# In the whole pairs the row sums' small additions, minima and squares run on GpSimd, in three instructions, in place of two on VectorE

## The chip, the cores and the metric

The kernel runs on one core of a Trainium2 chip. The metric is the device time of one execution in microseconds. The core's engines run side by side, each through its own instructions in a fixed order, and wait for one another through semaphores: TensorE (PE, with its weight loads as PEld), VectorE (DVE), ScalarE (ACT), GpSimd (POOL), and SyncE (SP), whose queue issues the DMA transfers.

## The reference

An attention with a threshold, whose output goes through a two-layer network with a leaky activation. There are 8 batches of 8 heads with 576 positions of 64 numbers, and 4608 tokens of 512 numbers.

```python
scores = scale * np.matmul(q, k.transpose(0, 1, 3, 2))
thresh = np.max(scores, axis=-1, keepdims=True) - tau
scores = np.where(scores >= thresh, scores, -1000000000.0)
scores = scores - np.max(scores, axis=-1, keepdims=True)
attn = np.exp(scores)
attn = attn / (np.sum(attn, axis=-1, keepdims=True) + 1e-09)
out = np.matmul(attn, v)                  # then (batch, seq, head) as x
h = x @ w_in
g = np.maximum(h, 0.0) + alpha * np.minimum(h, 0.0)
y = g @ w_out
```

## The kernel before

Two heads of a batch make a pair; there are 32 pairs. A pair is worked in nine units of 128 score rows (`UNITS`), so the attention has 288 units, and a loop over cycles `i` emits the work around one unit per cycle. The order in which it emits is the order in which PE, DVE, ACT and POOL run their instructions (`manual_schedule`); SP's queue is ordered by the scheduler.

For a unit, PE computes the scores `s` in one of two PSUM buffers (line 441), DVE takes the row maximum `nmx` (line 456), ACT computes the exponentials `p` and the threshold `thr` (lines 464 and 469), and DVE masks `p` by the threshold and accumulates the row sum into a column of the pair's tile `sm` (line 476, called the mask below). The mask is the last reader of `s`, so PE may fill that buffer again only behind it. PE transposes `p` (line 485), and ACT or DVE carry the result to SBUF (lines 558 and 561 in the whole pairs). PE multiplies it with the values (`av`, line 620).

A pair's nine columns of sums become the factors by which its output is scaled: `recip` computes `rv` from `sm`, PE transposes `rv` one cycle later (`rp`, line 643), ACT copies it (line 647), SP sends it out to DRAM and back as `rb`, and POOL multiplies the output `xa` with it, five cycles behind the transpose.

The first five pairs (0 to 4) are "whole" (`WHOLE = 5`): their probabilities are kept in one float32 part, with a share `SHARE / S` added to each (lines 558 and 561), and their factor is min(sum, 1) times the sum, inverted. The other 27 pairs split the probabilities in two parts, and their factor is the sum inverted. `recip` of a whole pair runs in cycle `o + 9`, where `o` is the pair's first cycle: the last mask of the pair lies one cycle earlier, and the mask and a row maximum of the next pair are emitted ahead of `recip`.

In the same cycles the weights of the second network are decoded from 64-bit words (`Split64`): loads, ACT lines 139, 140 and 160, the DVE lines 143 (clamp), 146 (shift), 151 (sign) and 156 (power) on SBUF tiles of 128x512, and on POOL the products, differences and sums of lines 164 to 168, each in two halves of 128x256, which the trace shows at line 77, the line of the helper (`wri`, `wti`, `wi` and `wro`, `wto`, `wo` are the tiles). POOL also subtracts the rounded keys and queries of a coming pair (`kl` and `qt`).

From cycle 45 on the network's first layers are woven between the units, and after the attention its other passes follow, with PE as the engine that all of them use.

Of the kernel before, what the change touches and what calls it, by code (L numbers as in the profile page):

```python
# [10 lines left out]
F32 = mybir.dt.float32  # L11
# [5 lines left out]
ALU = mybir.AluOpType  # L17
# [4 lines left out]
P = 128  # L22
# [58 lines left out]
def tile_masked_attention_moe(  # L81
# [11 lines left out]
    nc = tc.nc  # L93
# [173 lines left out]
    ap1 = at.enter_context(tc.tile_pool(name="ap1", bufs=1))  # L267
# [35 lines left out]
    class Pair:  # L303
# [329 lines left out]

        def recip(self):
            self.rv = ap1.tile([P, 9], F32, tag="rv", name=f"rv{self.pi}", bufs=2)
            nc.vector.tensor_scalar(self.rv, self.sm, 1e-9, None, op0=ALU.add)
            if self.whole:
                nc.vector.scalar_tensor_tensor(self.rv, self.rv, 1.0, self.rv, op0=ALU.min, op1=ALU.mult)
            nc.vector.reciprocal(self.rv, self.rv)

        def rturn(self):
# [617 lines left out]
```

## Time and profile before

| | |
|---|---|
| median of 3 runs | 1360.91 us (1358.39 to 1362.42) |
| profiled execution | 1360.37 us, span 1358.6 us |
| PE busy | 1324.9 us, 98% of the span |
| PEld busy | 1162.3 us, 86% |
| DVE busy | 973.6 us, 72% |
| ACT busy | 842.4 us, 62% |
| POOL busy | 970.8 us, 71% |

The span runs from the first to the last instruction of one profiled execution; its own time is 1.8 us longer. A busy time counts the instructions' own durations, waits inside an instruction included. Times in the rows below are microseconds from the start of the span.

### The profile page before, as it was taken

Reading aid. Unit: us, or ns where it says so; the run is one execution under the profiler, and the core shown is the slowest. Engines: PE = TensorE matmul, PEld = TensorE weight load, DVE = VectorE, ACT = ScalarE, POOL = GpSimd, SP = SyncE. Lnnn points to the kernel's source line nnn. Section 1 sums busy time; section 2 is a strip of 40 time slices with the busy share of each in tenths; the row PEclk is TensorE's granted clock in tenths of the full one; section 3 lists DMA queues with packets and bytes.
Section 4 is the critical chain, followed back from the end, with each engine's and each line's share of the span. In section 5 each row is a group of like instructions: output and inputs, shape, how many; then the busy total and the mean of one; then the engine's idle time right before and its main releaser. Section 6 shows DMA issues by size and latency. Waiting matters only on the chain.

```text
span 1358.6 us, 24051 instructions
## 1 busy us (share of the span) xinstructions
PE 1324.9 (98%) x8041; PEld 1162.3 (86%) x8041; DVE 973.6 (72%) x1843; ACT 842.4 (62%) x1910; POOL 970.8 (71%) x1369
## 2 busy tenths in 40 slices
PE   6988999999999999999999999999999999999999
PEld 4655799999999999999999999988888888888887
DVE  6989889889888888888888874665565744333332
ACT  7888888888888888888888873433332321211110
POOL 3766899899889898988988985775665754433431
PEclk9999999999999999999999999999999999999999
DMA  8653544644544645545445414345555443343222
GB/s 241 183 160 104 152 131 121 166 128 120 160 134 124 165 127 142 140 132 144 141 136 146 117 51 127 109 132 170 183 164 196 134 145 124 109 152 113 93 78 86
DMA packets 113595, 186.04 MB, mean 137 GB/s; under 512 B 16608, under 2 KB 47872, under 8 KB 113472
## 3 DMA queue, kind: packets, MB, share of 16 engines
q1 hardware_dynamic: 113152, 183.92, 46.2%
q8 instruction: 64, 1.05, 0.3%
q10 hardware_dynamic: 320, 0.59, 0.2%
q14 instruction: 59, 0.48, 0.1%
HBM read 104.41 MB, written 37.90 MB: 105 GB/s over the span
## 4 chain that ended last, share of the span: by engine, by line
PE 83%; DVE 6%; ACT 6%; POOL 1%; DMA 1%; issue 1%; ACTq 0%; SPq 0%; POOLq 0%; DVEq 0%
PE acca L256 12%; PE pha L226 12%; PE s L441 10%; PE phc L226 9%; PE av L620 8%; PE accc L256 8%; PE accb L256 7%; PE phb L226 7%; PE t L485 7%; DVE p L476 2%; DVE nmx L456 2%; PE tk L501 1%; PE accc L981 1%; ACT p L464 1%; ACT xh L205 1%
## 5 line engine op out<-in xcount | busy, mean ns | idle before, releaser
L456 DVE TENSOR_REDUCE nmx<-s 128x1 f32<-128x576 f32 x288 | 217.2, 754 | 67.8 <-PE s L441 65.3
L256 PE MATMUL acca<-wo,ga 128*128 128x512 f32 x756 | 224.1, 415 | 0.9 <-ACT xb L631 0.9
L476 DVE SCALAR_TENSOR_TENSOR p<-s,thr,p 128x576 f32<-128x576 f32 x256 | 206.6, 807 | 4.5 <-ACT thr L469 4.4
L464 ACT ACTIVATE p<-s,nmx 128x576 f32<-128x576 f32 x256 | 189.8, 741 | 8.7 <-DVE nmx L456 8.4
L441 PE MATMUL s<-kh,qst 128*128 128x288 f32 x640 | 141.6, 311 | 27.9 <-DVE p L476 16.2
L250 POOL TENSOR_TENSOR gc<-ptc,gc 128x512 fp32r<-128x512 f32 x45 | 58.1, 1292 | 144.0 <-ACT gc L247 144.0
L226 PE MATMUL pha<-xh,wi 128*128 128x256 f32 x784 | 157.9, 285 | 0.2 <-ACT pra L239 0.2
L485 PE MATMUL t<-ident,p 128*128 128x128 f32 x1024 | 154.5, 273 | 0.0
L247 ACT ACTIVATE gc<-ptc 128x512 fp32r<-128x512 f32 x45 | 28.4, 632 | 196.8 <-DVE ptc L951 196.8
L256 PEld LDWEIGHTS acca<-wo,ga 128*128 128x128 f32 x756 | 133.5, 190 | 19.1 <-ACT xb L631 1.4
L441 PEld LDWEIGHTS s<-kh,qst 128*128 128x128 f32 x640 | 100.1, 191 | 54.6 <-issue 26.4
L226 PEld LDWEIGHTS pha<-xh,wi 128*128 128x128 f32 x784 | 128.0, 190 | 6.5 <-ACT pra L239 3.6
L441 PE MATMUL s<-kl,qst 128*128 128x288 f32 x640 | 133.1, 298 | 0.0
L485 PEld LDWEIGHTS t<-ident,p 128*128 128x128 f32 x1024 | 124.4, 141 | 1.3 <-DVE e L551 1.0
L942 POOL TENSOR_TENSOR homexl<-homexr,homexh 128x512 fp32r<-128x512 f32 (+1 forms) x84 | 103.2, 1247 | 22.1 <-ACT homexh L941 22.0
L226 PE MATMUL phc<-homexh,wi 128*128 128x512 f32 x360 | 112.5, 389 | 0.0
L226 PE MATMUL pha<-xl,wi 128*128 128x256 f32 x392 | 110.7, 283 | 0.0
L578 POOL TENSOR_TENSOR rt<-kw,rt 64x128 fp32r<-64x128 f32 x216 | 97.8, 453 | 17.3
L256 PE MATMUL accc<-wo,gc 128*128 128x512 f32 x480 | 110.1, 389 | 0.0
L250 POOL TENSOR_TENSOR ga<-pta,ga 128x256 fp32r<-128x256 f32 x126 | 96.0, 763 | 18.5 <-ACT ga L247 10.1
L256 PEld LDWEIGHTS accc<-wo,gc 128*128 128x128 f32 x480 | 90.1, 188 | 18.7
L551 DVE TENSOR_TENSOR eo<-t,eo 128x512 fp32r<-128x512 f32 (+1 forms) x162 | 94.7, 598 | 12.7 <-ACT eo L547 11.5
(160 smaller groups left out, 3345.2 us busy)
## 6 DMA issues: line engine op xcount, KB each, us to landing
kr<-in_k_dram SPq DMA_DIRECT2D x31, 320.0 KB
rb<-rvd SPq DMA_DIRECT2D x64, 144.0 KB
xs<-xa SPq DMA_DIRECT2D x32, 288.0 KB
pinb<-part SPq DMA_DIRECT2D x36, 256.0 KB
part<-obb SPq DMA_DIRECT2D x36, 256.0 KB
pinc<-part SPq DMA_DIRECT2D x36, 256.0 KB
out_dram<-obc SPq DMA_DIRECT2D x35, 256.0 KB
qr<-in_q_dram SPq DMA_DIRECT2D x31, 288.0 KB
```

What stands on the lines that cost most here:

```text
L226: nc.tensor.matmul(ph[:, :n], w[:, c, :], xx[:, c, :n], start=(c == 0 and ti == 0), stop=(c == NCC - 1 and ti == 2),)
L250: nc.gpsimd.tensor_tensor(g[:, 1, :n], t[:, :n], f(g[:, 0, :n]), op=ALU.subtract)
L256: nc.tensor.matmul(acc[:m, :], gg[:, g, o : o + m], w, start=(first and ti == 0), stop=(last and ti == 2))
L441: nc.tensor.matmul(ps[:, h, :288], w, kk[:, a + h * 288 : a + (h + 1) * 288], start=(ki == 0 and i == 0), stop=(ki == 1 and i == n - 1),)
L456: nc.vector.tensor_reduce(self.nmx[:, j : j + 1], self.S[u][0][:, :, :288], axis=AX.XY, op=ALU.max, negate=True)
L464: nc.scalar.activation(pj, ps[:, :, :288], AF.Exp, bias=nmx[:, j : j + 1], scale=1.0)
L476: nc.vector.scalar_tensor_tensor(pj, ps[:, :, :288], thr[:, j : j + 1], pj, op0=ALU.is_ge, op1=ALU.mult, accum_out=self.sm[:, c : c + 1])
L485: nc.tensor.transpose(tb[:, c, :], pt[:, j, j * D + c * P : j * D + (c + 1) * P], ident)
L551: nc.vector.tensor_tensor(dst[1], ps, f(dst[0]), op=ALU.subtract)
L578: nc.gpsimd.tensor_tensor(lo, r, f(hi), op=ALU.subtract)
L620: nc.tensor.matmul(pa[:m, :n], w, x, start=(part == 0 and c == 0), stop=c == NKC)
L942: self.low.tensor_tensor(xl[:, c, :n], xr[:, c, :n], f(xh[:, c, :n]), op=ALU.subtract)
```

## The change

`recip` builds `rv` for a whole pair from three GpSimd instructions: one adds 1e-9 and takes the minimum with 1 into a new tile `ru`, one adds 1e-9 into `rv`, and one multiplies the two. The reciprocal stays on VectorE. The other pairs keep the addition on VectorE.

```diff
         def recip(self):
             self.rv = ap1.tile([P, 9], F32, tag="rv", name=f"rv{self.pi}", bufs=2)
-            nc.vector.tensor_scalar(self.rv, self.sm, 1e-9, None, op0=ALU.add)
             if self.whole:
-                nc.vector.scalar_tensor_tensor(self.rv, self.rv, 1.0, self.rv, op0=ALU.min, op1=ALU.mult)
+                ru = ap1.tile([P, 9], F32, tag="ru", name=f"ru{self.pi}", bufs=1)
+                nc.gpsimd.tensor_scalar(ru, self.sm, 1e-9, 1.0, op0=ALU.add, op1=ALU.min)
+                nc.gpsimd.tensor_scalar(self.rv, self.sm, 1e-9, None, op0=ALU.add)
+                nc.gpsimd.tensor_tensor(self.rv, self.rv, ru, op=ALU.mult)
+            else:
+                nc.vector.tensor_scalar(self.rv, self.sm, 1e-9, None, op0=ALU.add)
             nc.vector.reciprocal(self.rv, self.rv)
```

On VectorE, at the end of pair 3, these rows stood before (the digit behind a name is the pair's or the weight's number, so `sm3` belongs to pair 3):

```order
L476 SCALAR_TENSOR_TENSOR p4_0_1323,sm4_1285<-s4_0_1286,thr4_0_1321,p4_0_1323 128x576
L561 TENSOR_SCALAR o110_135<-t3_8_1326 128x4x128
L636 TENSOR_SCALAR rv3_1371<-sm3_995 128x9
L638 SCALAR_TENSOR_TENSOR rv3_1371<-rv3_1371 128x9
L639 RECIPROCAL rv3_1371<-rv3_1371 128x9
L156 TENSOR_SCALAR wro3_1168<-wto3_1248 128x512
L143 TENSOR_SCALAR wto4_1345<-wto4_1345 128x512
L476 SCALAR_TENSOR_TENSOR p4_0_1323,sm4_1285<-s4_1_1315,thr4_0_1321,p4_0_1323 128x576
L456 TENSOR_REDUCE nmx4_2_1390<-s4_2_1355 128x1
```

And these stand there now:

```order
L476 SCALAR_TENSOR_TENSOR p4_0_1329,sm4_1291<-s4_0_1292,thr4_0_1327,p4_0_1329 128x576
L561 TENSOR_SCALAR o110_135<-t3_8_1332 128x4x128
L643 RECIPROCAL rv3_1377<-rv3_1377 128x9
L156 TENSOR_SCALAR wro3_1174<-wto3_1254 128x512
L143 TENSOR_SCALAR wto4_1351<-wto4_1351 128x512
L476 SCALAR_TENSOR_TENSOR p4_0_1329,sm4_1291<-s4_1_1321,thr4_0_1327,p4_0_1329 128x576
L456 TENSOR_REDUCE nmx4_2_1398<-s4_2_1361 128x1
```

The reciprocal has kept its place, behind the two removed instructions' neighbours, and now waits for POOL instead of for VectorE itself.

On GpSimd, at the end of pair 4, these rows stood before (`kl6` and `qt6` prepare pair 6, `wro5`, `wto5` and `wo5` are a weight's decode):

```order
L375 TENSOR_TENSOR kl6_1596<-kr6_1536,kh6_1594 128x640
L77 TENSOR_TENSOR wro5_1348<-wro5_1348 128x256 x2
L77 TENSOR_TENSOR wto5_1452<-wto5_1452,wo5_1564 128x256 x2
L77 TENSOR_TENSOR wo5_1564<-wto5_1452,wro5_1348 128x256 x2
L403 TENSOR_TENSOR qt6_1690<-qr6_1626,qst0_111 128x576
```

And these stand there now:

```order
L375 TENSOR_TENSOR kl6_1604<-kr6_1544,kh6_1602 128x640
L77 TENSOR_TENSOR wro5_1354<-wro5_1354 128x256 x2
L77 TENSOR_TENSOR wto5_1460<-wto5_1460,wo5_1572 128x256 x2
L77 TENSOR_TENSOR wo5_1572<-wto5_1460,wro5_1354 128x256 x2
L638 TENSOR_SCALAR ru4_1665<-sm4_1291 128x9
L639 TENSOR_SCALAR rv4_1664<-sm4_1291 128x9
L640 TENSOR_TENSOR rv4_1664<-rv4_1664,ru4_1665 128x9
L403 TENSOR_TENSOR qt6_1700<-qr6_1634,qst0_111 128x576
```

The three new instructions stand behind the key difference and the three steps of a weight's decode, and ahead of the query difference. In pair 3 they stand at the same place, in pair 2 behind `kl` and `wi`, and in pairs 0 and 1 behind `wri` and `wti` and ahead of `wi`. The order of all other instructions on PE, ACT, DVE and POOL is the same in both kernels; on SP some neighbours have changed places.

## Rows read from the trace of the kernel before

**Rows 1.** The page's part 4, the chain of work that ended last, its shares by engine.

```profile
PE 83%; DVE 6%; ACT 6%; POOL 1%; DMA 1%; issue 1%; ACTq 0%; SPq 0%; POOLq 0%; DVEq 0%
```

**Rows 2.** Busy time by stretch, the stretch from 150 us to the end: start and end, its length, busy time of PE, PEld, DVE, ACT and POOL with their instructions, granted clock, DMA share and GB/s.

```profile
150.00:1358.60 1208.60, 1198.86 (x7379) 1077.04 (x7377) 846.72 (x1601) 718.92 (x1644) 877.89 (x1231) 1.00 0.45 133
```

**Rows 3.** The waits from 25 to 150 us: who waited for whom, us in total, times, longest.

```profile
PE s L441 <- DVE p L476: 10.3, 12, 2.3
POOL kl L77 <- ACT kh L368: 9.3, 3, 4.9
...
POOL kl L375 <- ACT kh L368: 8.1, 2, 4.9
```

**Rows 4.** The instructions that write the tile `rv`: line, engine, operation, count, shortest, median and longest duration in ns, first and last start.

```profile
L636 DVE TENSOR_SCALAR rv<-sm x32: 158/278/798, 36.6 to 810.9; 128x9 f32<-128x9 f32 x32
L639 DVE RECIPROCAL rv<-rv x32: 215/216/218, 37.8 to 811.2; 128x9 f32<-128x9 f32 x32
...
L638 DVE SCALAR_TENSOR_TENSOR rv<-rv x5: 532/657/677, 37.1 to 138.0; 128x9 f32<-128x9 f32 x5
```

**Rows 5.** The time line at the end of pair 0: start, duration, engine, line, instruction, and in brackets the idle time before it and what ended it. DVE first, then POOL, then PE.

```profile
37.78 0.21 DVE L639 RECIPROCAL rv<-rv 128x9 f32<-128x9 f32 x1
37.91 1.05 DVE L151 SCALAR_TENSOR_TENSOR wti<-wri,wti 128x512 int32<-128x512 int32 x1
...
36.30 1.42 POOL L77 TENSOR_TENSOR wti<-wti,wi 128x256 f32<-128x256 f32 x2
...
40.51 0.50 PE L441 MATMUL s<-kh,qst 128*128 128x288 f32 x2 [0.92 <-DVE p L476]
```

**Rows 6.** The time line at the end of pair 1, DVE and POOL.

```profile
62.66 0.22 DVE L639 RECIPROCAL rv<-rv 128x9 f32<-128x9 f32 x1
...
60.47 1.41 POOL L77 TENSOR_TENSOR wti<-wti,wi 128x256 f32<-128x256 f32 x2
```

**Rows 7.** The time line at the end of pair 2, DVE and POOL.

```profile
87.81 0.22 DVE L639 RECIPROCAL rv<-rv 128x9 f32<-128x9 f32 x1
...
85.19 1.42 POOL L77 TENSOR_TENSOR wi<-wti,wri 128x256 fp32r<-128x256 f32 x2
```

**Rows 8.** The time line at the end of pair 3, DVE, then POOL, then PE.

```profile
112.02 0.53 DVE L636 TENSOR_SCALAR rv<-sm 128x9 f32<-128x9 f32 x1
112.59 0.66 DVE L638 SCALAR_TENSOR_TENSOR rv<-rv 128x9 f32<-128x9 f32 x1
113.28 0.21 DVE L639 RECIPROCAL rv<-rv 128x9 f32<-128x9 f32 x1
113.41 0.81 DVE L156 TENSOR_SCALAR wro<-wto 128x512 int32<-128x512 int32 x1
114.13 1.60 DVE L143 TENSOR_SCALAR wto<-wto 128x512 f32<-128x512 f32 x1
115.66 0.80 DVE L476 SCALAR_TENSOR_TENSOR p<-s,thr,p 128x576 f32<-128x576 f32 x1
...
112.47 1.43 POOL L77 TENSOR_TENSOR wo<-wto,wro 128x256 fp32r<-128x256 f32 x2
113.87 1.58 POOL L403 TENSOR_TENSOR qt<-qr,qst 128x576 fp32r<-128x576 f32 x1
115.42 1.36 POOL L77 TENSOR_TENSOR wro<-wro 128x256 f32<-128x256 f32 x2
...
116.61 0.50 PE L441 MATMUL s<-kh,qst 128*128 128x288 f32 x2 [2.33 <-DVE p L476]
```

**Rows 9.** The time line at the end of pair 4, DVE (its first row is the last mask of pair 4), then POOL, then PE.

```profile
133.82 0.81 DVE L476 SCALAR_TENSOR_TENSOR p<-s,thr,p 128x576 f32<-128x576 f32 x1
...
138.72 0.22 DVE L639 RECIPROCAL rv<-rv 128x9 f32<-128x9 f32 x1
138.85 1.05 DVE L151 SCALAR_TENSOR_TENSOR wto<-wro,wto 128x512 int32<-128x512 int32 x1
...
140.49 0.80 DVE L476 SCALAR_TENSOR_TENSOR p<-s,thr,p 128x576 f32<-128x576 f32 x1
...
138.62 1.87 POOL L77 TENSOR_TENSOR wo<-wto,wro 128x256 fp32r<-128x256 f32 x2
140.65 1.41 POOL L403 TENSOR_TENSOR qt<-qr,qst 128x576 fp32r<-128x576 f32 x1 [0.15 <-ACT qr L393]
...
141.45 0.50 PE L441 MATMUL s<-kh,qst 128*128 128x288 f32 x2 [1.04 <-DVE p L476]
```

**Rows 10.** The time line of POOL, three of its short instructions.

```profile
143.49 0.45 POOL L578 TENSOR_TENSOR rt<-kw,rt 64x128 fp32r<-64x128 f32 x1
...
172.16 0.18 POOL L662 TENSOR_TENSOR xa<-xa,xb 64x1 f32<-64x1 f32 x1
172.43 0.21 POOL L663 TENSOR_SCALAR vs<-xa 64x1 f32<-64x1 f32 x1
```

**Rows 11.** Two lines of the weights' decode on DVE: count, shortest, median and longest duration in ns.

```profile
L143 DVE TENSOR_SCALAR wto<-wto x7: 409/422/1602, 75.6 to 132.0; 128x512 f32<-128x512 f32 x7
...
L151 DVE SCALAR_TENSOR_TENSOR wti<-wri,wti x7: 681/689/1273, 20.5 to 72.9; 128x512 int32<-128x512 int32 x7
```

**Rows 12.** Busy time by stretch, from 20 to 30 us, with columns as in rows 2, and the PE time line in that stretch.

```profile
20.00:30.00 10.00, 8.03 (x44) 6.93 (x45) 8.98 (x17) 8.65 (x21) 6.25 (x8) 0.83 0.93 241
...
23.29 0.58 PE L441 MATMUL s<-kh,qst 128*128 128x288 f32 x2 [1.94 <-DVE p_t L476]
```

## Prediction

> **What bounds the kernel now.** I read the shares of the chain that ended last first [rows 1]: PE holds 83% of it, DVE and ACT 6% each. Then the busy time by stretch: from 150 us to the end PE is busy 1198.86 of 1208.60 us [rows 2], so nothing that reaches PE late there is made good by waiting less; PE's order is fixed, and a shift at 150 us is a shift at the end. The whole pairs lie before 150 us, and the waits of 25 to 150 us say what holds PE there [rows 3]: 12 times, 10.3 us in all, the next scores `s` wait for a mask on DVE. DVE is the engine to watch in this stretch, and the time lines at the ends of the five whole pairs show what stands around `rv` on it [rows 5 to 9].
>
> **What is removed.** Two DVE instructions in each of five pairs, ten in all. They look dear for nine columns: the addition took 0.53 us and the minimum and square 0.66 us in pair 3 [rows 8], where the shortest addition of this kind took 0.158 and none of the five squares less than 0.532 [rows 4]. From the addition's start to the reciprocal's start it is 113.28 - 112.02 = 1.26 us there. If DVE simply went on without them, five pairs would save at most 5 x 1.26 = 6.3 us. But the reciprocal stays in its place on DVE and now waits for POOL, and DVE takes its instructions in order: behind the reciprocal stand a step of a weight's decode, a row maximum and a mask, and for that mask PE waits. So what counts is not the work that leaves DVE but when POOL finishes the three instructions, against when the reciprocal started before.
>
> **What three POOL instructions cost.** POOL has no addition of 128x9 in the trace. The nearest rows are an addition of 64x1, 0.18 us, and a scaling of 64x1, 0.21 us, 0.27 us from start to start [rows 10]. Three in a row take 0.27 + 0.27 + 0.20 = 0.74 us; the hand-over to DVE I put at 0.11 us, under the 0.16 us from the end of a mask (140.49 + 0.80 = 141.29) to the PE start at 141.45 that waited for it [rows 9]. So the reciprocal starts about 0.85 us after POOL has reached the three. Bounds: three times 0.18, with no gaps, is 0.55; three times the 0.45 us of a 64x128 subtraction [rows 10] plus 0.16 is 1.5. I take 0.85, since nine columns are nearer to one than to 128.
>
> **When POOL gets there.** POOL does not wait for the sums: pair 4's last mask ends at 133.82 + 0.81 = 134.63 [rows 9], some 4 us before the reciprocal. It is POOL's own queue that is late. It idles until ACT has rounded a coming pair's keys (17.4 us in five waits [rows 3]), and then works off `kl` and the weight's steps without a pause; each pair starts such a block anew, so lateness in one pair is not carried into the next one's block. The three stand behind that work:
> - Pair 0: POOL is free of `wti` at 36.30 + 1.42 = 37.72 [rows 5]; the reciprocal starts at 38.57 instead of 37.78, 0.79 us late.
> - Pair 1: 60.47 + 1.41 = 61.88 [rows 6]; 62.73 instead of 62.66, 0.07 late.
> - Pair 2: 85.19 + 1.42 = 86.61 [rows 7]; 87.46 instead of 87.81, 0.35 early.
> - Pair 3: 112.47 + 1.43 = 113.90 [rows 8]; 114.75 instead of 113.28, 1.47 late.
> - Pair 4: `wo` took 1.87 us while DVE's line 151 ran beside it; with DVE waiting I give it pair 3's 1.43, so 138.62 + 1.43 = 140.05 [rows 8, 9]; 140.90 instead of 138.72, 2.18 late.
>
> Bare lateness: 0.79 + 0.07 - 0.35 + 1.47 + 2.18 = 4.16 us.
>
> **What the next DVE instruction then meets.** In pair 3 the lines 156 and 143 took 0.81 and 1.60 us, where line 143 takes 0.409 at its shortest [rows 8, 11]. They ended 0.32 us after POOL's `wo` (114.22 against 113.90) and 0.28 us after `qt` (115.73 against 115.45) [rows 8]: they could only start when POOL's instruction was over. The reciprocal is never so held, 0.215 to 0.218 us in all 32 [rows 4]. Now POOL starts its next instruction as soon as the three are done, ahead of DVE's next one, so each time that one must let POOL's go first:
> - Pair 0: POOL's first half of `wi`, 0.68 us (half of pair 3's 1.36 [rows 8]), runs to 37.72 + 0.74 + 0.68 = 39.14; line 151 ends some 0.6 us later (0.689 less its front of 0.1 [rows 11]), 39.74 against 37.91 + 1.05 = 38.96: 0.8 late.
> - Pair 3: `qt` runs from 114.64 for 1.41 us [rows 9] to 116.05; line 156 ends at 116.4, POOL's first half of `wro` takes 0.68, and line 143 ends 0.28 later, at 117.3 against 115.73: 1.6 late.
> - Pair 4: `qt` runs from 140.79 to 142.20; line 151 ends at 142.8 against 138.85 + 1.05 = 139.90: 2.9 late.
> - Pairs 1 and 2: I leave 0.1 late and 0.35 early.
>
> This agrees with a rule of the Trainium skill (GPSIMD Engine Reference, section 1, Specifications): GpSimd's SBUF interfaces are shared with VectorE, and contention comes with VectorE instructions in a two-port mode or with two SBUF inputs. By it the sum is the one below; without it, it is the bare 4.16.
>
> **The sum.** 0.8 + 0.1 - 0.35 + 1.6 + 2.9 = 5.05 us later masks. Does PE take all of it? Behind pairs 0, 3 and 4 PE already waits for exactly the mask that stands behind the reciprocal, 0.92, 2.33 and 1.04 us [rows 5, 8, 9], so these pass in full. The other costs I put at nothing: POOL's 0.74 us delay `wi` and `qt`, which PE needs cycles later (pair 4's `qt` prepares pair 6); if that cover were gone it would be 5 x 0.74 = 3.7 us at most. The transpose of `rv` stands on PE a cycle behind, after scores that wait for the late mask anyway. SP's changed neighbours are the same transfers, some issued one place earlier or later, with POOL's multiplication by `rb` five cycles behind the transpose as cover. The profiled execution took 1360.37 us, 0.54 under the median of the runs: 1360.37 + 5.05 = 1365.4 us. Its own range, with 0.55 to 1.5 for the three and with or without the second effect: 4.16 - 5 x 0.3 = 2.7 at the low end, 5.05 + 5 x 0.65 = 8.3 at the high end, 1363.1 to 1368.7.
>
> **The rivals.**
> - *VectorE is relieved in time* (other side). If POOL came to the three before DVE is done with its row maximum, each pair would save what the addition and square took, up to 1.26 us; 6.3 in all, 1354.1 us. The point of decision is the reciprocal's old start: POOL must be free 0.85 us before it. It is so in pair 2 alone, by 0.35 us; in pair 4 it misses by 2.2. For it speaks that spans on POOL are rough; if all pairs did as pair 2, 5 x 0.35 gives 1358.6. Chance 0.07.
> - *The lateness is taken up.* ACT or PE might be the later one at some of these places, so that half or less passes: 0 to 2.5 us, 1360.4 to 1362.9. Against it: the waits of PE named above, and PE's 1198.86 of 1208.60 afterwards [rows 2]. For it: pair 1's and 2's waits are not pinned down so well. Chance 0.23.
> - *TensorE's clock falls in the longer waits.* From 20 to 30 us the granted clock was 0.83, after a wait of 1.94 us at 23.29 [rows 12]: with the low level at half, 10 x 0.17 / 0.5 = 3.4 us were spent at 1.2 GHz, costing up to 1.7 us. In pair 3 a wait of 2.33 us sat in a row with full-speed scores (0.50 us [rows 8], against 0.58 at 23.29), so one such wait need not do it. After the change these waits would be 2.33 + 1.6 = 3.9 and 1.04 + 2.9 = 3.9 us. One fall gives 1367.1, two 1368.8. Chance 0.2.
>
> Forecast as summed: 0.5.
>
> **The numbers.** The likeliest is 1365.4. About 0.3%, 4.1 us, is what a measurement of this kernel can tell from no change. Slower by more than that needs a sum above 4.1: the forecast's case does so in some three of four (0.38) and the clock's case always (0.2), 0.58. Faster by more than that needs most of the first rival's 6.3 us: 0.03. The rest, 0.39, lies within. The range reaches from the upper half of the case in which the lateness is taken up to two falls of the clock: 1361.5 to 1369.0.
>
> **What the profile after would show.** The reciprocal waits for POOL's multiplication of `rv`, with DVE idle ahead of it: 114.75 - 112.02 = 2.7 us in pair 3, where DVE was free when the addition began [rows 8], some 2.18 + 1.1 = 3.3 in pair 4, under half a microsecond in pair 2. The three POOL instructions take about 0.2 us each. DVE's line 151 or 156 behind the reciprocal ends with POOL's `qt`. PE's waits for the mask in pairs 3 and 4 grow to nearly 4 us, and everything from 150 us on is moved by about 5 us, with PE's busy time unchanged. Wrong would make it: three POOL instructions far from 0.74 us; `kl` on POOL starting earlier against DVE than before; or a wait of PE that grows while the end does not move.

## The result, and the profile after

The changed kernel takes 1368.39 us (median of 4 runs, 1367.18 to 1368.53), the kernel before 1360.54 us beside it (4 runs, 1358.39 to 1362.42). The ratio is 1.0056, its 95% interval 1.0039 to 1.0074: slower by 7.9 us, more than the 4.1 us that the prediction asked for. The sign and the way the masks come late are as forecast; the time is 3.0 us above the forecast 1365.4. It lies inside the range only because the range reaches up to the rival of the falling clock, which had a chance of 0.2. The runs below show that this rival took part.

The profiled execution took 1368.53 us, 8.16 more than the one of before. First the busy times of the page and the chain that ended last:

```profile
PE 1327.4 (97%) x8041; PEld 1164.0 (85%) x8041; DVE 971.1 (71%) x1833; ACT 842.5 (62%) x1910; POOL 973.9 (71%) x1384
...
PE 84%; ACT 6%; DVE 4%; POOL 3%; issue 2%; DMA 1%; ACTq 0%; POOLq 0%; DVEq 0%
```

DVE gave up ten instructions, and its busy time fell by 2.5 us only (973.6 before): lines that were held got longer. In the chain DVE has 4% instead of 6%, POOL 3% instead of 1% [rows 1].

The waits from 25 to 150 us, who waited for whom, us in total, times, longest; the second row is new:

```profile
PE s L441 <- DVE p L476: 14.7, 12, 4.0
...
DVE rv L643 <- POOL rv L640: 9.7, 5, 3.4
```

PE's waits for the mask were 10.3 us with a longest of 2.3 [rows 3]; they have grown by 4.4 us, still in 12 places. Behind 150 us little is made good. This is the busy time by stretch, columns as in [rows 2], from 150 us to the end; then four short stretches at the ends of pairs 3 and 4, whose last number but two is the granted clock:

```profile
150.00:1366.50 1216.50, 1206.72 (x7419) 1081.82 (x7417) 853.84 (x1610) 723.88 (x1656) 884.92 (x1243) 1.00 0.45 132
...
115.00:120.00 5.00, 1.91 (x11) 1.25 (x10) 3.50 (x7) 1.84 (x4) 4.41 (x8) 1.00 0.56 159
120.00:125.00 5.00, 5.00 (x24) 3.62 (x23) 4.21 (x8) 4.31 (x11) 2.42 (x4) 0.66 0.38 121
...
145.00:150.00 5.00, 1.66 (x7) 1.67 (x8) 5.00 (x10) 1.62 (x4) 1.25 (x1) 0.82 0.75 186
150.00:155.00 5.00, 5.00 (x26) 3.19 (x25) 2.74 (x6) 3.30 (x8) 3.64 (x8) 0.84 0.01 2
```

From 150 us to the end PE idles 9.78 us, as the 9.74 of [rows 2]: a shift at 150 us reaches the end but for some 0.5 us. At 120 and at 145 us the clock is below 1.00; in the kernel before all stretches of this size from 110 to 155 us show 1.00.

The end of pair 3, POOL, then DVE, then PE (start, duration, instruction, idle time before it and what ended it). It answers to [rows 8]:

```profile
114.09 1.43 POOL L77 TENSOR_TENSOR wo<-wto,wro 128x256 fp32r<-128x256 f32 x2
115.60 0.27 POOL L638 TENSOR_SCALAR ru<-sm 128x9 f32<-128x9 f32 x1
115.93 0.24 POOL L639 TENSOR_SCALAR rv<-sm 128x9 f32<-128x9 f32 x1
116.26 0.21 POOL L640 TENSOR_TENSOR rv<-rv,ru 128x9 f32<-128x9 f32 x1
116.42 1.40 POOL L403 TENSOR_TENSOR qt<-qr,qst 128x576 fp32r<-128x576 f32 x1
118.18 1.29 POOL L77 TENSOR_TENSOR wro<-wro 128x256 f32<-128x256 f32 x2 [0.36 <-DVE wro L156]
...
116.50 0.22 DVE L643 RECIPROCAL rv<-rv 128x9 f32<-128x9 f32 x1 [2.51 <-POOL rv L640]
116.63 1.47 DVE L156 TENSOR_SCALAR wro<-wto 128x512 int32<-128x512 int32 x1
118.02 0.41 DVE L143 TENSOR_SCALAR wto<-wto 128x512 f32<-128x512 f32 x1
118.36 0.81 DVE L476 SCALAR_TENSOR_TENSOR p<-s,thr,p 128x576 f32<-128x576 f32 x1
...
119.32 0.50 PE L441 MATMUL s<-kh,qst 128*128 128x288 f32 x2 [3.09 <-DVE p L476]
```

DVE sits idle for 2.51 us until POOL has gone through `wo` and the three. Line 156 then ends at 118.10, 0.28 us after POOL's `qt` (116.42 + 1.40 = 117.82), the same 0.3 us behind as before. PE's wait has grown from 2.33 us to 3.09.

The end of pair 4, POOL, DVE, PE, against [rows 9]:

```profile
144.68 0.21 POOL L640 TENSOR_TENSOR rv<-rv,ru 128x9 f32<-128x9 f32 x1
144.85 1.40 POOL L403 TENSOR_TENSOR qt<-qr,qst 128x576 fp32r<-128x576 f32 x1
...
144.92 0.22 DVE L643 RECIPROCAL rv<-rv 128x9 f32<-128x9 f32 x1 [3.38 <-POOL rv L640]
145.05 1.74 DVE L151 SCALAR_TENSOR_TENSOR wto<-wro,wto 128x512 int32<-128x512 int32 x1
147.38 0.80 DVE L476 SCALAR_TENSOR_TENSOR p<-s,thr,p 128x576 f32<-128x576 f32 x1
...
148.34 0.82 PE L441 MATMUL s<-kh,qst 128*128 128x288 f32 x2 [4.01 <-DVE p L476]
```

PE waits 4.01 us where it waited 1.04, and the scores behind the wait take 0.82 us instead of 0.50: the clock has fallen.

**Where the time went.** I set each mask's start against that of the same mask before, all 288. The shift is 1.06 us before the first changed instruction has run; it goes to 1.83 over pair 0, stays there over pairs 1 and 2 (1.88 ahead of pair 3's reciprocal), goes to 2.70 with pair 3's late mask (118.36 against 115.66) and to 3.92 at low clock behind it, to 6.89 with pair 4's late mask (147.38 against 140.49), to 8.41 at low clock, and is 7.92 at the last mask; most of the 0.5 in between is given back from 375 to 410 us. So the late masks cost 0.77 + 0.82 + 2.99 = 4.6 us, the two low clocks 1.22 + 1.52 = 2.7 us. The 1.06 of the start belongs to this execution: other executions of the same or nearly the same code, below, start with -0.5 to 1.5.

### The profile page after: what moved, and what is told of

It reads as the page before. It is cut to its first block, busy times and chain, and to the rows that moved or that the text cites. A ratio compares the mean times of both kernels' runs of the same rounds, so it can differ in the third digit from the quotient of the medians.

```text
span 1366.5 us, 24055 instructions
## 1 busy us (share of the span) xinstructions
PE 1327.4 (97%) x8041; PEld 1164.0 (85%) x8041; DVE 971.1 (71%) x1833; ACT 842.5 (62%) x1910; POOL 973.9 (71%) x1384
## 3 DMA queue, kind: packets, MB, share of 16 engines
q8 instruction: 64, 1.05, 0.3%
## 4 chain that ended last, share of the span: by engine, by line
PE 84%; ACT 6%; DVE 4%; POOL 3%; issue 2%; DMA 1%; ACTq 0%; POOLq 0%; DVEq 0%
PE acca L256 12%; PE pha L226 12%; PE s L441 10%; PE phc L226 9%; PE av L620 8%; PE accc L256 8%; PE accb L256 7%; PE phb L226 7%; PE t L485 7%; DVE p L476 1%; DVE nmx L456 1%; PE tk L501 1%; PE accc L985 1%; ACT p L464 1%; ACT xh L205 1%
```

## The experiments

The kernel before ran beside each group of kernels. Its medians are 1359.98 us (15 runs) beside the changes in pairs 0 to 2 and in pair 4, the unaltered kernel and the one with nine products; 1359.87 (24 runs) beside the one with eleven and eighteen products, the two with the sums on neither engine or on both, and the reciprocal one cycle later; 1359.99 (21 runs) beside the other three. "Shift" always means a mask's start against the same mask in the profile of the kernel before.

### The change in pairs 0 to 2 alone

```diff
-            if self.whole:
+            if self.whole and self.pi < 3:
...
+                if self.whole:
+                    nc.vector.scalar_tensor_tensor(self.rv, self.rv, 1.0, self.rv, op0=ALU.min, op1=ALU.mult)
```

> The three GpSimd instructions stand in pairs 0, 1 and 2 alone; pairs 3 and 4 are as in the kernel before. If each pair pays by how late GpSimd comes to the three, only pair 0 is late: about +0.8 us, 1361.3 against 1360.5. If the 1.0 us that the first 20 us took longer in the changed kernel belong to the change, +1.8. If all five pairs pay alike (8 us over five), +4.8.

Measured: 1361.2 us (1358.85 to 1363.06, 11 runs), ratio 1.0007 [0.9998 to 1.0015]. The shift is 1.02 at the start, 1.79 over pair 0, 1.80 behind pair 1, 1.6 to 2.0 behind pair 2 and 1.25 at the end. So pair 0 costs 0.8 us, and pairs 1 and 2 next to nothing; the three pairs together hold only a small part of the 7.9 us.

### The change in pair 4 alone

```diff
-            if self.whole:
+            if self.whole and self.pi == 4:
...
```

The second half of the edit is that of the kernel above: the other whole pairs keep the minimum and square on VectorE.

> The three GpSimd instructions stand in pair 4 alone. By lateness: the mask behind the reciprocal 2.95 us late, and a fall of TensorE's clock behind a wait of 4 us that costs another 1.5: +4.4 us, about 1364.9. If lateness alone counts and the clock stays up: +2.9. If all five pairs pay alike: +1.6.

Measured: 1366.1 us (1365.56 to 1366.88, 5 runs), ratio 1.0045 [1.0033 to 1.0058]; one pair makes most of the loss. Two waits of PE and two stretches of it:

```profile
116.75 0.78 PE L441 MATMUL s<-kh,qst 128*128 128x288 f32 x2 [1.99 <-DVE p L476]
145.85 0.82 PE L441 MATMUL s<-kh,qst 128*128 128x288 f32 x2 [4.05 <-DVE p L476]
...
115.00:120.00 5.00, 3.25 (x12) 2.54 (x13) 4.84 (x9) 1.95 (x6) 4.86 (x7) 0.68 0.62 174
145.00:150.00 5.00, 4.15 (x13) 2.73 (x13) 3.73 (x8) 3.02 (x7) 1.21 (x4) 0.50 0.36 117
```

The late mask adds 3.0 us (shift 1.39 to 4.40), the clock behind it 2.35 (to 6.75): from 145 to 150 us all of it is at the lower level, 1.2 GHz. The first row was not expected: pair 3 is as before here, its wait of 1.99 us is shorter than the 2.33 of [rows 8], and yet the clock fell and cost 1.0 us. So a low clock behind such a wait is not the change's alone; it comes in some executions. In the runs of the kernel before, too, the granted clock averaged over the span goes from 0.997 to 1.000.

### The changed kernel again, and with TensorE kept at work

The first kernel of the three is the changed one, unaltered. The other two add products of the identity with itself, whose result nothing reads, at the ends of pairs 3 and 4, ahead of the scores that wait for the late masks (`filler.run` exists in the kernel for other cycles; in the trace each product is two matmuls); nothing else differs.

```diff
+            if i in (36, 45):
+                filler.run(9)
```

and in the third

```diff
+            if i in (36, 45):
+                filler.run(11 if i == 36 else 18)
```

> The changed kernel once more beside the others: about 1368.4 us. Its first mask starts as late against the kernel before as in the first profile (0.7 us) if that belongs to the change, and by another amount if it is the spread of the start.

> The changed kernel with nine filler products on TensorE (some 2.5 us, results unused) at the place where TensorE waits in pairs 3 and 4. If the falls of the clock behind those waits cost 1.2 and 1.5 us, the clock stays at full in both and the time is 2.7 us under the changed kernel, about 1365.7. If the low clock there is hidden by other waits, no gain: 1368.4 or more.

> As e_fill, with eleven filler products in pair 3's wait and eighteen in pair 4's, so that TensorE waits no more than a microsecond or so in either. If the low clock behind those waits is the rest of the loss, the clock stays full from 110 to 160 us, the masks behind pair 4 are 0.8 + 1.0 + 2.9 = 4.7 us late and not 7.2, and the time is some 2.5 us under the changed kernel's. If the low clock costs nothing, the time is the changed kernel's.

Measured: unaltered 1367.24 us (1366.25 to 1368.28), ratio 1.0053 [1.0039 to 1.0067]; nine products 1366.97 us (1366.64 to 1367.46), 1.0051 [1.0038 to 1.0064]; eleven and eighteen 1365.11 us (1364.28 to 1366.17), 1.0035 [1.0021 to 1.0049]; 5 runs each.

The unaltered kernel: its waits of PE in pairs 3 and 4, and the stretches behind them:

```profile
118.55 0.50 PE L441 MATMUL s<-kh,qst 128*128 128x288 f32 x2 [3.31 <-DVE p L476]
146.36 0.82 PE L441 MATMUL s<-kh,qst 128*128 128x288 f32 x2 [4.03 <-DVE p L476]
...
120.00:125.00 5.00, 4.94 (x26) 3.03 (x25) 4.29 (x9) 4.95 (x13) 2.63 (x5) 1.00 0.35 118
145.00:150.00 5.00, 3.64 (x13) 2.73 (x13) 3.99 (x9) 2.68 (x6) 0.78 (x3) 0.50 0.46 125
```

Here the clock held behind 3.31 us and fell behind 4.03 us. With nine products, a wait of 2.02 us was left in pair 4, and the clock fell behind that too, so the 1365.7 us expected of it did not come:

```profile
146.45 0.83 PE L441 MATMUL s<-kh,qst 128*128 128x288 f32 x2 [2.02 <-DVE p L476]
...
145.00:150.00 5.00, 3.55 (x12) 2.71 (x13) 4.07 (x9) 2.58 (x6) 0.72 (x2) 0.66 0.50 125
```

With eighteen, PE has no wait there, and the clock stays at 1.00:

```profile
140.96 4.18 PE L695 MATMUL filler<-ident 128*128 128x128 f32 x36
146.51 0.53 PE L441 MATMUL s<-kh,qst 128*128 128x288 f32 x2
...
145.00:150.00 5.00, 5.00 (x31) 3.52 (x30) 4.38 (x10) 3.37 (x8) 1.50 (x5) 1.00 0.45 128
```

The masks are as late as ever: the shift goes from 2.14 to 5.15 over pair 4, from 1.93 to 4.91 in the unaltered kernel; what is missing is the step to 7.21 behind it. So the clock is worth about 1367.24 - 1365.11 = 2.1 us and the late masks the rest, 1365.11 - 1359.87 = 5.2 us, of which up to 0.2 may be products that outlasted the wait. The intervals of the two ratios overlap, but the runs do not: all nine of the unaltered kernel, 1366.25 us or more, are above all five with eighteen products, 1366.17 or less. The clock averaged over the span goes the same way: 0.995 to 0.997 in those nine runs, 0.999 to 1.000 in the five.

### The sums on neither engine, and on GpSimd beside VectorE

The first kernel leaves out the addition, the minimum and the square in the whole pairs; there `rv` is the reciprocal of the sums as they are. The second keeps VectorE's two instructions and adds the three of GpSimd on tiles that nothing reads. Both edits are against the kernel before.

```diff
+            if self.whole:
+                nc.vector.reciprocal(self.rv, self.sm)
+                return
             nc.vector.tensor_scalar(self.rv, self.sm, 1e-9, None, op0=ALU.add)
-            if self.whole:
-                nc.vector.scalar_tensor_tensor(self.rv, self.rv, 1.0, self.rv, op0=ALU.min, op1=ALU.mult)
             nc.vector.reciprocal(self.rv, self.rv)
```

```diff
             nc.vector.tensor_scalar(self.rv, self.sm, 1e-9, None, op0=ALU.add)
             if self.whole:
...
+                nc.gpsimd.tensor_scalar(ru, self.sm, 1e-9, 1.0, op0=ALU.add, op1=ALU.min)
+                nc.gpsimd.tensor_scalar(rw, self.sm, 1e-9, None, op0=ALU.add)
+                nc.gpsimd.tensor_tensor(rw, rw, ru, op=ALU.mult)
                 nc.vector.scalar_tensor_tensor(self.rv, self.rv, 1.0, self.rv, op0=ALU.min, op1=ALU.mult)
```

> The kernel before without the addition, the minimum and the square in the whole pairs (left out, rv is the sums inverted), on no engine: what VectorE's relief is worth by itself. If the 1.1 to 1.3 us between a row maximum and the reciprocal lie on the chain in all five pairs, some 5 us faster, 1355; if the next instruction then waits for GpSimd's port in their place, 1 to 3 us; if they were hidden, no change.

> The kernel before, with the three GpSimd instructions added in the same places on tiles that nobody reads; VectorE computes rv as before. If GpSimd's 0.8 us of work by themselves delay nothing, the time of the kernel before, within 1 us. If they do (keys, queries, weights later, or VectorE held at the port), +0.7 to +3.7 us.

Measured: without them 1356.86 us (1355.48 to 1357.75, 8 runs), ratio 0.9976 [0.9966 to 0.9986]; with both 1358.22 us (1356.63 to 1360.23, 11 runs), 0.9984 [0.9975 to 0.9993].

The relief of VectorE is real, 3.0 us, if nothing takes its place: half of the 6.3 us that the prediction gave for every pair saving pair 3's 1.26. It comes mainly from pair 3 (-1.9 us); pairs 1 and 2 give 0.5 each. Not all of pair 3's gain is the two instructions: its late mask comes 2.1 us earlier (0.2 is lost again behind it), and 0.85 of that is in lines 156 and 143, which take 0.62 and 0.96 us there instead of 0.81 and 1.60 [rows 8].

And GpSimd's 0.9 us per pair, put on its queue, cost nothing on balance: what costs is that the reciprocal waits for them. That this kernel is even 1.65 us faster than before I had not expected. Its minimum and square on VectorE; then, in pair 3, POOL's first short instruction, VectorE's lines 156 and 143, and PE's wait:

```profile
L643 DVE SCALAR_TENSOR_TENSOR rv<-rv x5: 170/171/656, 38.3 to 137.6; 128x9 f32<-128x9 f32 x5
...
114.45 0.52 POOL L640 TENSOR_SCALAR ru<-sm 128x9 f32<-128x9 f32 x1
114.55 0.37 DVE L156 TENSOR_SCALAR wro<-wto 128x512 int32<-128x512 int32 x1
114.84 0.41 DVE L143 TENSOR_SCALAR wto<-wto 128x512 f32<-128x512 f32 x1
...
116.13 0.50 PE L441 MATMUL s<-kh,qst 128*128 128x288 f32 x2 [0.70 <-DVE p L476]
```

The minimum and square took 0.532 at least and 0.657 in the median before [rows 4]; in pairs 0 to 2 it now takes 0.17, beside short POOL instructions. In pair 3, where most of the gain lies, it still takes 0.65 us, beside the long `wo`. What is shorter there are the two lines behind it: they take 0.37 and 0.41 us instead of 0.81 and 1.60 [rows 8] and end at 115.25, before POOL's `qt` starts at 115.60. PE's wait is 0.70 instead of 2.33 us (the profiled execution is this kernel's slowest, with a shift of 1.5 us at the start, and yet has it). That POOL's three short instructions stand between two long ones and let VectorE in is the reading that fits; no run tests it by itself.

### The three one cycle earlier on GpSimd

The three are emitted right behind the pair's last mask instead of a cycle later; the reciprocal and all behind it stay. On POOL they then stand behind `kl` in pairs 0 and 1, in pair 2 where they stood, and ahead of `wo` in pairs 3 and 4.

(`sums` holds what stood in `recip` ahead of the reciprocal.)

```diff
...
         if p.whole:
+            first_at_cycle(o + fin[0] - 1, p.sums)
         at_cycle(o + fin[0], p.recip)
```

> As the changed kernel, with the three on POOL emitted one cycle earlier, right behind the pair's last mask; the reciprocal and all behind it stay where they are. On POOL they then stand behind kl in pairs 0 and 1, behind wto in pairs 3 and 4. If the whole loss comes from POOL's place in its queue: POOL is free by about 35.0, 59.2, 85.2 to 86.6, 112.5 and 138.7 us, the reciprocal (0.98 us later) comes earlier than before in pairs 0 and 1, within 0.2 in pair 3 and some 0.9 us late in pair 4, where up to 0.7 more may come of the held line 151; no clock falls. Sum -2 to +1 us, 1358 to 1361 us. If the loss comes from the POOL instructions themselves or from the hand-over between the engines, wherever they stand: 1365 to 1367 us as the changed kernel.

Measured: 1361.05 us (1360.21 to 1361.99, 11 runs), ratio 1.0009 [1.0 to 1.0018]. The reciprocals in pairs 3 and 4:

```profile
113.81 0.21 DVE L647 RECIPROCAL rv<-rv 128x9 f32<-128x9 f32 x1 [1.12 <-POOL rv L640]
139.58 0.21 DVE L647 RECIPROCAL rv<-rv 128x9 f32<-128x9 f32 x1 [1.98 <-POOL rv L640]
```

The shift is 0.6 just ahead of pair 3's reciprocal and about 0 ahead of pair 4's, so the first is within 0.1 us of its old place and the second 0.9 us late against [rows 8, 9], as expected; the mask behind pair 4's is 0.9 us late. The shift starts at 1.01 and is 0.62 at the end. The same instructions on the same engines, with one step of POOL's queue fewer ahead of them in pairs 3 and 4 (`wo`) and two in 0 and 1: the loss is gone but for what cannot be told from none. It was the place in the queue.

### The reciprocal one cycle later

```diff
-FINW = (9, 10, 11, 14, 16, 17, 18)
+FINW = (9, 11, 12, 14, 16, 17, 18)
...
         if p.whole:
+            at_cycle(o + fin[0] + 1, p.invert)
```

Here the three stay on POOL as in the changed kernel; VectorE's reciprocal, PE's transpose and ACT's copy each come a cycle later.

> The changed kernel with the whole pairs' reciprocal one cycle later on VectorE, behind the next mask, and the transpose and the copy of rv one cycle later each. If VectorE's wait for GpSimd is what costs, it is gone: the masks are at or ahead of the kernel before, 1355 to 1361 us. If GpSimd's longer queue costs by itself, or the clock falls anyway, it stays 2 us or more above the kernel before.

Measured: 1360.75 us (1359.02 to 1363.65, 11 runs), ratio 1.0007 [0.9999 to 1.0016]. DVE waits for POOL once, 0.2 us:

```profile
DVE rv L647 <- POOL rv L640: 0.2, 1, 0.2
```

The loss is gone here too, but what VectorE was relieved of is not left either. The shift is 0.2 behind pair 0, -1.7 behind pair 3 and still -1.7 at 180 us; at 185 us it is +0.5. The token load `xr` is late there. In this kernel, SP's issue of the load and POOL's first instruction on it, then VectorE's line 682, which stands ahead of a row maximum:

```profile
148.65 0.59 SPq L200 DMA_DIRECT2D xr<-xs  x1
154.80 0.40 POOL L214 CAST xh<-xr 128x256 fp32r<-128x256 f32 x1 [3.54 <-DMA xr<-xs]
...
182.19 0.62 DVE L682 TENSOR_SCALAR rb<-rb,vs 128x576 f32<-128x576 f32 x1 [1.92 <-POOL xa L679]
```

and in the kernel before:

```profile
148.04 0.59 SPq L200 DMA_DIRECT2D xr<-xs  x1
153.16 0.40 POOL L214 CAST xh<-xr 128x256 fp32r<-128x256 f32 x1 [0.42 <-DMA xr<-xs]
```

SP issues `xr` behind pair 4's `rb`, which now leaves a cycle later. POOL waits 3.54 us instead of 0.42, runs on without a pause from there, and at 182 us VectorE waits for it. The next two kernels try this reading.

### Two ways to keep the transfers early

The first takes the reciprocal a cycle later and has ACT copy in its old cycle; the second takes it later in pairs 0 to 3 and leaves pair 4 as before the change. Both edits are shown against the kernel just above.

```diff
-FINW = (9, 11, 12, 14, 16, 17, 18)
+FINW = (9, 11, 11, 14, 16, 17, 18)
```

```diff
-            if self.whole:
+            if self.whole and self.pi < 4:
...
-        fin = FINW if p.whole else FINS
+        fin = FINS if not p.whole else FINW if p.pi < 4 else FINV
```

(`FINV` is the old `FINW`.)

> As the kernel with the reciprocal a cycle later (1360.75 us), but ACT copies the transposed factors in the cycle in which it did so before. In the later one the masks stood 1.7 us ahead of the kernel before until 180 us and 0.5 behind from 185 us on: POOL waited 3.54 us for the token load xr, which SP issued at 148.65 behind pair 4's rb (147.50), and VectorE then waited 1.92 us for POOL. If it is that one later cycle in SP's queue that gave the gain back, rb and xr go out some 2 us earlier, POOL's wait falls under 1.5 us, and the time is about 1358.7 us (1358.0 to 1359.6). Rival: ACT, now close behind the transpose, waits for it and hands the delay on, or the backlog on POOL has another cause: 1360 to 1361.5.

> As the kernel with the reciprocal a cycle later, in pairs 0 to 3 alone; pair 4 is as in the kernel before, with its two instructions on VectorE and its transfers in their old cycle. If the token load behind pair 4's rb gave the gain back, xr is issued some 1.7 us earlier than in the kernel before, the 2.1 us at 183 us do not come, and the time is about 1358.5 us (1357.8 to 1359.5). Rival: the backlog has another cause than pair 4's transfers, and the time stays at 1360 to 1361.5.

Measured: 1368.43 us (1367.23 to 1369.13, 5 runs), ratio 1.0063 [1.005 to 1.0075], and 1360.47 us (1358.84 to 1360.85, 11 runs), ratio 0.9998 [0.9989 to 1.0007].

In the first the rival came true, and at a higher price than I gave it. The waits from 25 to 160 us:

```profile
ACT rt L655 <- PE rp L651: 11.1, 5, 3.3
```

ACT, which has exponentials of the next units queued behind the copy, stands still five times for a transpose that comes late in the same cycle; the shift grows by 0.5 to 3.2 us in every whole pair. Part of that is the clock again, behind the copies of pairs 2 and 3; from 105 to 110 us it is nearly all at the lower level:

```profile
105.00:110.00 5.00, 5.00 (x16) 3.11 (x17) 3.15 (x8) 3.93 (x8) 1.35 (x2) 0.52 0.15 60
```

In the second the late load is mended (line numbers are one higher):

```profile
147.56 0.59 SPq L201 DMA_DIRECT2D xr<-xs  x1
152.13 0.40 POOL L215 CAST xh<-xr 128x256 fp32r<-128x256 f32 x1 [0.40 <-DMA xr<-xs]
```

The shift is -1.02 behind pair 4 and stays so to the last mask (-1.04): the step at 183 us has not come. With the chain in the rows above this speaks for the token load; since all of pair 4 is as before here, and not the load alone, it is not shown apart from the rest of that pair. The expected 1358.5 us did not come out: about 1.0 us was given back by 840 us, behind the last mask, where this execution has a wait of PE for ACT of 0.74 us at 822.24 us that neither the kernel before nor the one with all five reciprocals late has. The profiled executions with nine and with eighteen products have the same wait of 0.74 us at the same place, 16.5 us behind the start of the last mask, and lose 1.05 us there, while the unaltered kernel's has neither; so it is no mark of the late reciprocal. What brings it stays open; nothing that can be told from the kernel before was gained.

## Why the prediction was right, and where it was off

**What bounds it: right, to about a microsecond.** PE's waits for the mask carried the shift, and a shift at 150 us reached the end but for two places where executions differ: up to 1.2 us is given back from 375 to 410 us, and up to 1.4 lost behind the last mask. In the kernels with late reciprocals further steps follow (2.1 us at 183 us).

**The place on POOL decides: right**, and shown from two sides: three instructions on POOL that nothing waits for cost nothing on balance, and one cycle earlier in POOL's queue the same change costs nothing that can be told.

**What the three cost: 0.85 us forecast, 0.98 measured** (115.52, when `wo` ends, to 116.50). The instructions are as forecast, 0.27, 0.24 and 0.21 us; the starts lie 0.33 us apart, where I took the 0.27 of [rows 10], and the first starts 0.08 after `wo`. The hand-over to DVE is 0.03 us instead of 0.11.

**The bare lateness by pair: right but for the shift it sits on.** With the shift of the mask ahead taken off, the reciprocals are late by 0.9, 0.2, -0.2, 1.3 and 2.3 us; the forecast was 0.79, 0.07, -0.35, 1.47 and 2.18. The first three of them after the change:

```profile
39.77 0.22 DVE L643 RECIPROCAL rv<-rv 128x9 f32<-128x9 f32 x1 [2.01 <-POOL rv L640]
64.67 0.21 DVE L643 RECIPROCAL rv<-rv 128x9 f32<-128x9 f32 x1 [1.24 <-POOL rv L640]
89.41 0.22 DVE L643 RECIPROCAL rv<-rv 128x9 f32<-128x9 f32 x1 [0.56 <-POOL rv L640]
```

**What the next DVE instruction meets: right in pairs 0 and 4, mis-sized in pair 3.** Lines 156 and 151 took 1.47 and 1.74 us instead of 0.81 and 1.05 and ended 0.28 and 0.54 us behind POOL's `qt`; the reciprocal ahead of them took its 0.22 as ever. This agrees with the rule of the Trainium skill that the prediction named (GPSIMD Engine Reference, section 1, Specifications), that GpSimd shares its SBUF interfaces with VectorE. Of the two conditions that the Trainium skill gives there for contention, line 151 meets the one of two SBUF inputs; line 156 reads one tile, and no row here shows whether it ran in a two-port mode. Masks were 0.77 and 2.99 us late there, forecast 0.8 and 2.9. In pair 3 it was 0.82 instead of 1.6: I let POOL's first half of `wro` run ahead of line 143 for 0.68 us. But line 156 writes `wro`; POOL had to wait 0.36 us for it and started at 118.18, and line 143 came first, at 118.02, and took 0.41 us, not held at all, where it took 1.60 before [rows 8]. With 0.8 in that term the sum is 4.25 us; pair 2's -0.35 was not kept either, which makes 4.6, as the masks show.

**That PE takes all of it: right** for the three pairs named. Pairs 1 and 2 neither lost nor gained. (POOL's multiplication by `rb` stands six cycles behind the transpose, 10 and 16 in `FINW`, not five; the cover that the sum counted on is a cycle longer than said.)

**The clock: the step that failed.** I gave 0.5 to the case in which it holds and 0.2 to the case in which it falls once or twice, 1367.1 and 1368.8. It fell twice in the profiled execution, and behind pair 4's late mask in all four profiles with waits of 2.02 to 4.05 us there; it held behind the 1.96 us that are left with the three one cycle earlier, and with eighteen products, where no wait is left. The argument was that a wait of 2.33 us in pair 3 stood before full-speed scores. One such row shows that a wait of that length need not bring the clock down; it says nothing on a wait of 4.0 us, and the price that I worked out from [rows 12], up to 1.7 us a fall, was near (1.22 and 1.52 here, up to 2.35 in others). Without the falls the forecast's size is met, 5.05 us forecast and 5.2 with PE kept at work, but partly by luck: pair 3's term was 0.8 us too large, pair 2's -0.35 did not come, and that kernel's profile loses 1.05 us behind the last mask and gets 1.2 us back before it, neither of which is in the sum.

**The other rivals.** VectorE was not relieved in time in pairs 3 and 4, and where it was, in pair 2, nothing was left of it at the end; the relief without any replacement is 3.0 us, not 6.3. The lateness was not taken up.

Most of the profile's marks came as written: the reciprocal's waits of 2.51 and 3.38 us (2.7 and 3.3 forecast), lines 156 and 151 ending just behind `qt`, PE's wait in pair 4 at 4.01 (3.9). In pair 3 it is 3.09 instead of 3.9, the mis-sized term. Three marks failed. PE's busy time was to stay; it is 1327.4 us instead of 1324.9, about what the two low clocks cost (2.7). The shift from 150 us on was to be about 5 us; it is 8.41. And pair 2's reciprocal waited 0.56 us, not under half a microsecond.

## What to carry to other kernels

Work that moves to another engine is to be priced by where that engine's queue stands when the result is wanted: here 0.9 us of work cost 5 us behind a long queue and nothing that can be told one step (pairs 3 and 4) or two (pairs 0 and 1) further ahead. A late link in such a chain has tails: TensorE's clock may fall in the longer wait, which cost some 40% on top here (2.1 us on 5.2), and a transfer queued behind a delayed one may hand the delay on 30 us later (here it fits the rows, and is not shown by itself). When the model lets one engine go ahead of another, ask whether its next instruction has its operands by then.

## What the runs showed of the hardware that I had not expected

- Most of what the two removed VectorE instructions took was not their own work: the minimum and square on nine columns takes 0.17 us when POOL's neighbours are short and 0.53 to 0.68 beside its long ones. The same holds of the decode's lines in pair 3, 0.37 and 0.41 us beside short ones, 0.81 and 1.60 beside long ones. In a profile such an instruction looks dear while its own work is small.
- The length of TensorE's wait did not by itself tell whether the clock fell: it fell behind 1.99 and 2.02 us and held behind 3.31 us and, in the kernel before, 2.33 us. What decided between them stays open.
- Ahead of the first changed instruction the executions shown here already differ by up to 2 us (shifts of -0.5 to 1.5); a loss of 1 us in one pair can be seen only mask by mask, not in the total.
